# Padded q, k, v weight blocks and a changed order of VectorE's work in a fused attention and gated feed-forward kernel

## The chip, the cores and the metric

The kernel runs on one core of a Trainium2 chip. The metric is device time in microseconds (us), from the first to the last instruction of an execution with what lies around it; lower is better. Everything is fp32; matrix products read their operands as `float32r`, each operand split into a high and a low part, with three products (high x high, high x low, low x high) for one.

## The reference

The input has 2048 rows of 640. Both branches read the same layer-normed rows:

```python
xn = _layernorm(x)
qkv = (xn @ wqkv)                        # 32 heads of 20
# each row attends to W=8 rows: itself and 2, 4, ... 14 rows before it
logits = einsum("bhsd,bhswd->bhsw", q, kg) * scale; masked where the row is before the first
o = einsum("bhsw,bhswd->bhsd", softmax(logits), vg)
s = o @ wo
h = (xn @ w_gate) * (xn @ w_up)          # 1536 wide
g = silu(h @ w_down)
out = x + s * g
```

## The kernel before

The rows are spread over 128 partitions, 16 to each. A *unit* is one head group (four groups of 5 heads, two of 6) for one parity of rows; there are 12 units, numbered 0 to 11, and units 8 to 11 have 6 heads. `unit(u)` makes q, k and v of eight tiles with `qkv` (L317: 15 products of 300 or 360 columns in one PSUM bank, tag "q", four banks in rotation); ScalarE copies k and v to `kv` (L319) and q to `q` (L320); two times in a unit SyncE's queue issues copies of `kv` one partition on (L324), so that each partition has its neighbour's rows. `attention(u)` is a generator with VectorE's work: products of q and k (L351), sums (L354), mask, maximum, difference (L361); the exponential on ScalarE (L363, with the sum on VectorE behind it at L365); weighted values (L372) and their sums (L380, L383).

Between units stand *pieces* of the gated part. `gate_up(f, ch)` makes one block of 128 columns for a quarter of the rows: 15 products for `g` and 15 for `u`, of 512 columns each (L96), in PSUM tiles with two buffers each. ScalarE copies `g` to `gs` (L420). The product `hs = u * gs` on VectorE (L431) is put off: `finish` is kept in `unfinished` until `finish_piece()` is called, in the next piece, at a unit's second tile or by hand. The `u` bank is free for the next piece but one when its `hs` is done.

The order on each engine is that of the program. VectorE's is set by credits: each piece and each qkv tile calls `advance(budget)`, which takes steps of the running attention while its estimated costs fit. So the order of `hs` among attention's steps follows from where the calls stand. The number of pieces behind a unit is a line of the main loop: three, and four behind units 2 and 5, the rest at the end. A weight block's split (high part on ScalarE L86, low part on GpSimd L87) is called in the second piece of the block before.

Behind the units come the last pieces (f0 = 10 and f1 = 11) by hand, with what the next stage wants: `turn_pair` turns two tiles of attention's output (L491, L744 to L747), `hi_pair` and `lo_pair` split them in three parts (L764 on ScalarE, L768 on VectorE), `sums_wo` and `sum_w5` (L706) make combinations of the output weights, `split_t` and `split_w5` split these. `pair_product(p, j)` (L789) makes seven products for a pair, in places A, C and B (banks q, u, g): the first in place A, the second in place C, which takes the `u` bank of piece (f1, 2), the third again in A, after ScalarE has copied the first (L792). Then follow single output tiles (L96 in `out_proj`) and the down projection (L660).

Tiles lie one behind another in a partition's memory in the order in which they are first asked for; `skip(n)` puts n bytes between them. `wqh` and `wql` hold a group's weight block, five rows of 300 or 360 columns.

Of the kernel before, what the change touches and what calls it, by code (L numbers as in the profile page):

```python
# [12 lines left out]
F32R = mybir.dt.float32r  # L13
AF = mybir.ActivationFunctionType
# [5 lines left out]
P = 128  # L20
# [6 lines left out]
KD, KF = D // P, F // P  # L27
# [24 lines left out]
def kernel(  # L52
# [11 lines left out]
    nc = tc.nc  # L64
# [11 lines left out]
    def st(shape, tag, bufs, dt=F32):  # L76
        cnt[0] += 1
        return sb.tile(shape, dt, tag=tag, bufs=bufs, name=f"{tag}_{cnt[0]}")
# [19 lines left out]
    def skip(n):  # L98

        cnt[0] += 1  # L100
        sb.tile([P, n // 4], F32, tag=f"skip_{cnt[0]}", bufs=1, name=f"skip_{cnt[0]}")


    wq_raw, wq = {}, {}
# [10 lines left out]
    def split_wq(g, eng, ks=(0, KD)):  # L115
        c3 = 3 * GROUPS[g] * DH
        if g not in wq:
            wq[g] = st([P, KD, c3], "wqh", 1, F32R), st([P, KD, c3], "wql", 1, F32R)
        for k0, k1, t in wq_raw[g]:
            if ks[0] <= k0 < ks[1]:  # L120
                split(eng, t, wq[g][0][:, k0:k1], wq[g][1][:, k0:k1])
# [48 lines left out]
    eps_t = st([P, 1], "eps", 1)  # L170
# [92 lines left out]
    def scales(s0):  # L263
        mv, mr = stat[s0]
        nc.vector.tensor_copy(mr[:, 0, :], mv[:, :, 0])
        rstd(mv[:, :, 1], mr[:, 1, :], TPC)
        own[s0] = st([P, NQ, 2, TPC], "own", 2)
        nc.vector.tensor_mul(own[s0], mr.unsqueeze(1).to_broadcast([P, NQ, 2, TPC]),
                             quarter.unsqueeze(2).unsqueeze(3).to_broadcast([P, NQ, 2, TPC]))

    def spread(s0):

        p = pt([P, NQ, 2, TPC], "q", 4)
        nc.tensor.matmul(p, sel, own[s0], start=True, stop=True)
        spread_t[s0] = st([P, NQ, 2, TPC], "mrq", 2)
        nc.scalar.activation(spread_t[s0], p, AF.Copy)
# [51 lines left out]
    def attention(u):  # L328
        g, r = UN[u]
# [31 lines left out]
        nc.vector.tensor_sub(lg, lg, sm[:, 0, :].unsqueeze(2).to_broadcast([P, NE * nh, W]))  # L361
        yield 3 * small
        nc.scalar.activation(e, lg, AF.Exp, scale=SCALE)  # L363
        yield small
        nc.vector.tensor_reduce(out=sm[:, 0, :], in_=e, op=ALU.add, axis=AX.X)  # L365
        nc.vector.reciprocal(sm[:, 1, :], sm[:, 0, :])
# [42 lines left out]
    def gate_up(f, ch, between=(), amid=(), part=None):  # L409
        if part is None:  # L410
            pp = [pt([P, CH], "g", 2), pt([P, CH], "u", 2)]
            c = slice(0, CH)
        else:
            pp, c = part, slice(CH // 2, CH)
        last = (f, ch) == (KF - 1, NCH - 1)
        gate_up_half(f, ch, 0, pp[0], c)
        for act in amid:
            act()
        gs = st([P, CH], "gs", 2)
        nc.scalar.activation(gs, pp[0], AF.Copy)  # L420
        for act in between:
            act()
        share = (c.stop - c.start) / CH
        finish_piece()
        advance(PACE * 3.25 * share)
        gate_up_half(f, ch, 1, pp[1], c)

        def finish():
            hs = st([P, CH], "hs", 2)
            if not last:  # L430
                nc.vector.tensor_mul(hs, pp[1], gs)  # L431
            else:
                nc.scalar.activation(hs, pp[1], AF.Copy)
                nc.gpsimd.tensor_mul(hs, hs, gs)
            nc.sync.dma_start(h_scr[ch * TPC:(ch + 1) * TPC, :, f, :].rearrange("t p c -> p t c"),
                              hs.rearrange("p (t c) -> p t c", c=P))

        unfinished.append(finish)
        if last:
            finish_piece()  # L440
        advance(PACE * 3.25 * share)
# [3 lines left out]
    def finish_piece():  # L445

        while unfinished:
            unfinished.pop(0)()
# [289 lines left out]
    def turn_pair(p):  # L738
        y = pair_y[p] = st([P, 2, KD, P], "ot", 2)
        for i in range(2):  # L740
            turn(y[:, i], 2 * p + i)
        s1, s2, s4 = (pair_raw[p][:, i * KS:(i + 1) * KS] for i in range(3))
        a11, a12, a21, a22 = (y[:, i, k:k + KS] for i in range(2) for k in (0, KS))
        nc.vector.tensor_add(s1, a21, a22)  # L744
        nc.vector.tensor_sub(s2, s1, a11)
        nc.vector.tensor_sub(s4, a12, s2)
        nc.vector.tensor_sub(a21, a11, a21)  # L747
# [18 lines left out]
    def lo_pair(p, part):  # L766
        z, raw = pair_z[p, part]
        nc.vector.tensor_sub(z[1], raw, z[0].bitcast(F32))  # L768
# [35 lines left out]
            nc.sync.dma_start(s_scr[2 * p + 1], yb)  # L804


    skip(192)
    begin_unit(0)
    skip(192)
    mask = st([1, NE, W], "mask", 1)  # L810
    nc.gpsimd.memset(mask, 0.0)
    for i in range(NE - 1):
# [57 lines left out]
    load_xq(12, 3, xa)  # L870
    load_xq(15, 1, xd)
    scales(12)
    gate_up(0, 1, amid=(lambda: spread(8),))
    trans_q(8)
    trans_q(9)
# [56 lines left out]
    piece()  # L932
    for u in range(2, len(UN)):
        unit(u)
        for _ in range(3 + (u in (2, 5)) if u + 1 < len(UN) else len(pieces)):
            if len(pieces) == 1:
                load_wf(f1)
            piece()
# [28 lines left out]
    begin_wd()  # L967
    split_t("T1", wd_big[0], 4)
    split_t("T2", wd_big[0], 6)
    for i in range(3):  # L970
        lo_pair(0, i)
    gate_up(f1, 2)
    turn_pair(1)
    split_t("T3", wd_big[1], 4)
    split_t("T4", wd_big[1], 6)
    load_wd(0)
    load_wd(1)
    begin_wd()
    finish_piece()
    sum_w5()  # L980
    split_w5()
    gate_up(f1, 3)
# [148 lines left out]
```

## Time and profile before

| | |
|---|---|
| median of 3 runs | 778.97 us (778.11 to 779.29) |
| profiled execution, whole | 780.43 us |
| its span, first to last instruction | 778.6 us |
| TensorE busy | 767.9 us, 99% |
| VectorE busy | 697.3 us, 90% |
| ScalarE, GpSimd busy | 235.2 us, 150.1 us |
| mean granted TensorE clock | 0.995 |

A row of a timeline has the start, the length, engine, line, operation, output and inputs, shapes and count; in brackets the idle time before it and what ended it. Lengths of TensorE's products overlap, so starts are compared. Lines are those of the program above.

### The profile page before, as it was taken

How to read it: one execution, taken by the hardware profiler on the slowest of the kernel's cores; microseconds unless marked ns; L12 is line 12 of the kernel's file. 1: busy time of each engine (PE TensorE's matmuls, PEld its weight loads, DVE VectorE, ACT ScalarE, POOL GpSimd, SP SyncE). 2: the span in 40 equal slices, each digit the busy share in tenths (PEclk: the TensorE clock that was granted, in tenths of full speed). 3: DMA queues.
4: the chain of work that ended last, by engine and by line, in shares of the span. 5: the costliest groups of instructions: out<-in, count | busy, mean ns of one | idle time of the engine just before them, and what ended most of it. 6: DMA issues, size and time to landing. Idle time of an engine off the chain costs nothing.

```text
span 778.6 us, 11229 instructions
## 1 busy us (share of the span) xinstructions
PE 767.9 (99%) x4408; PEld 707.5 (91%) x4408; DVE 697.3 (90%) x731; ACT 235.2 (30%) x537; POOL 150.1 (19%) x114
## 2 busy tenths in 40 slices
PE   8999999999999999999999999999899999999997
PEld 7989899898989898989898989888799999999997
DVE  7899899999999999997999999999986787777775
ACT  4324312031112121312121212113455564444442
POOL 5200401022023101210204010034456720000000
PEclk9999999999999999999999999999999999999999
DMA  8552131321224122333032231444467674555533
GB/s 325 168 191 77 49 90 44 96 90 48 85 50 124 49 64 82 98 83 79 29 108 70 60 88 50 128 123 104 138 191 227 205 264 162 198 188 183 183 102 135
DMA packets 82252, 93.97 MB, mean 121 GB/s; under 512 B 23112, under 2 KB 63384, under 8 KB 82072
## 3 DMA queue, kind: packets, MB, share of 16 engines
q1 hardware_dynamic: 82200, 93.27, 38.7%
q8 instruction: 34, 0.56, 0.3%
q14 instruction: 18, 0.15, 0.1%
HBM read 55.84 MB, written 28.31 MB: 108 GB/s over the span
## 4 chain that ended last, share of the span: by engine, by line
PE 67%; DVE 24%; issue 5%; DMA 1%; ACT 1%; POOL 1%; DVEq 0%; SPq 0%; ACTq 0%; POOLq 0%
PE q L317 19%; PE q L660 11%; PE u L96 10%; PE g L96 10%; PE u L660 5%; PE q L96 5%; DVE t L351 4%; DVE t L380 4%; DVE t L372 4%; PE g L660 3%; DVE lg L354 2%; PE q L789 2%; DVE hs L431 2%; DVE xc L221 1%; PE u L789 1%
## 5 line engine op out<-in xcount | busy, mean ns | idle before, releaser
L96 PE MATMUL u<-xc,wf 128*128 128x512 f32 (+1 forms) x735 | 171.9, 386 | 0.4 <-DVE hs L431 0.4
L96 PE MATMUL g<-xc,wf 128*128 128x512 f32 (+1 forms) x735 | 172.1, 386 | 0.0
L317 PE MATMUL q<-wqh,xc 128*128 128x300 f32 (+1 forms) x960 | 161.6, 312 | 0.3
L96 PEld LDWEIGHTS u<-xc,wf 128*128 128x128 f32 x735 | 136.0, 188 | 28.0 <-DVE hs L431 0.8
L96 PEld LDWEIGHTS g<-xc,wf 128*128 128x128 f32 x735 | 135.7, 188 | 26.7
L317 PEld LDWEIGHTS q<-wqh,xc 128*128 128x128 f32 x960 | 147.0, 189 | 2.6 <-ACT wqh L86 0.4
L351 DVE TENSOR_TENSOR t<-q,kv 128x1600 f32<-128x1600 f32 (+1 forms) x48 | 98.7, 2055 | 6.2 <-DMA kv<-kv 6.2
L87 POOL TENSOR_TENSOR wf<-wraw,wf 128x256 fp32r<-128x256 f32 (+2 forms) x22 | 47.6, 2183 | 266.4 <-ACT wf L86 229.4
L372 DVE TENSOR_TENSOR t<-e,kv 128x1600 f32<-128x1600 f32 (+1 forms) x48 | 97.7, 2053 | 1.1
L354 DVE TENSOR_REDUCE lg<-t 128x80 f32<-128x1600 f32 (+1 forms) x48 | 92.6, 1929 | 1.1
L317 PE MATMUL q<-wql,xc 128*128 128x300 f32 (+1 forms) x480 | 87.2, 312 | 0.0
L420 ACT ACTIVATE gs<-g 128x512 f32<-128x512 f32 x48 | 28.6, 597 | 192.5 <-PE g L96 175.9
L380 DVE TENSOR_TENSOR t<-t,t 128x1600 f32<-128x1600 f32 (+1 forms) x36 | 78.8, 2190 | 1.0
L317 PEld LDWEIGHTS q<-wql,xc 128*128 128x128 f32 x480 | 75.4, 191 | 0.0
L319 ACT ACTIVATE kv<-q 128x200 f32<-128x200 f32 (+1 forms) x96 | 33.4, 348 | 125.2 <-PE q L317 125.2
L660 PE MATMUL q<-xc,wf 128*128 128x320 f32 x432 | 67.2, 309 | 0.0
L87 POOL TENSOR_TENSOR wql<-wraw,wqh 128x300 fp32r<-128x300 f32 (+4 forms) x14 | 35.3, 2539 | 165.6 <-ACT wqh L86 165.4
L660 PEld LDWEIGHTS q<-xc,wf 128*128 128x128 f32 x432 | 64.3, 188 | 0.0
L431 DVE TENSOR_TENSOR hs<-u,gs 128x512 f32<-128x512 f32 x47 | 32.0, 681 | 0.0
L87 POOL TENSOR_TENSOR xc<-wraw,xc 128x320 fp32r<-128x320 f32 (+1 forms) x22 | 26.2, 1193 | 28.5 <-ACT xc L86 25.4
L320 ACT ACTIVATE q<-q 128x100 f32<-128x100 f32 (+1 forms) x96 | 24.9, 259 | 0.0
L623 DVE TENSOR_TENSOR wf<-t,wf 128x768 fp32r<-128x768 f32 x16 | 15.3, 956 | 8.2 <-ACT wf L619 7.5
(259 smaller groups left out, 913.0 us busy)
## 6 DMA issues: line engine op xcount, KB each, us to landing
h_scr<-hs SPq DMA_DIRECT2D x48, 256.0 KB, 2.2
wraw<-in_wgu SPq DMA_DIRECT2D x12, 640.0 KB, 5.1
t<-h_scr SPq DMA_DIRECT2D x8, 768.0 KB, 7.0
hs<-s_scr SPq DMA_DIRECT2D x16, 320.0 KB, 3.5
gs<-in_x SPq DMA_DIRECT2D x16, 320.0 KB, 4.0
out<-q SPq DMA_DIRECT2D x14, 320.0 KB, 2.7
wraw<-h_scr SPq DMA_DIRECT2D x11, 384.0 KB, 5.9
wraw<-in_wd SPq DMA_DIRECT2D x12, 320.0 KB, 3.8
```

The lines of the kernel that those rows point to most:

```text
L87: eng.tensor_sub(lo, raw, hi.bitcast(F32))
L96: nc.tensor.matmul(acc, a, b, start=first and n == 0, stop=last and n == len(runs) - 1)
L317: nc.tensor.matmul(p, xT[(r * NE + i) // TPC][a][:, k, t0:t0 + P], wq[g][b][:, k], start=n == 0, stop=n == len(runs) - 1, skip_group_check ...
L319: nc.scalar.activation(kv_t[u][:, :, W - 1 + i, :], p[:, c:].rearrange("p (a c) -> p a c", a=2), AF.Copy)
L320: nc.scalar.activation(q_t[u][:, i, :], p[:, :c], AF.Copy)
L351: nc.vector.tensor_mul(t, q.rearrange("p i c -> p (i c)").unsqueeze(1).to_broadcast([P, 2, NE * c]), places(0, j))
L354: nc.vector.tensor_reduce(out=lg[:, :, j:j + 2].rearrange("p n a -> p a n"), in_=heads(t), op=ALU.add, axis=AX.X)
L372: nc.vector.tensor_mul(heads(t), pw, heads(places(1, j)))
L380: nc.vector.tensor_add(acc, acc, t)
L420: nc.scalar.activation(gs, pp[0], AF.Copy)
L431: nc.vector.tensor_mul(hs, pp[1], gs)
L660: nc.tensor.matmul(p, y[:, i, k], wd_t[name][k][:, l], start=new and r == 0, stop=r == len(runs) - 1, skip_group_check=True)
```

## The change

It has six edits.

1. The tiles `wqh` and `wql` get rows of 320 or 384 columns, of which 300 or 360 are used, so that each row of weights starts at a multiple of 256 bytes. The bytes skipped ahead are changed (192 and 192 to 32 and 160), which moves `q` and `kv` from 160 bytes past such a multiple onto one, and `wqh` and `wql` as well. The tile of edit 3 moves `lg`, `e` and `sm` to 32 bytes past one.
2. In `attention`, `finish_piece()` is called right behind the exponential.
3. An exponential of one column is run on ScalarE behind `scales(12)`.
4. The fourth piece is behind units 2 and 8, not 2 and 5.
5. `finish_piece()` for piece (f1, 2) is called right behind that piece, not behind `turn_pair(1)` and the splits.
6. `lo_pair(0, 2)` is moved behind that call.

```diff
     def split_wq(g, eng, ks=(0, KD)):
         c3 = 3 * GROUPS[g] * DH
         if g not in wq:
-            wq[g] = st([P, KD, c3], "wqh", 1, F32R), st([P, KD, c3], "wql", 1, F32R)
+            cols = -(-c3 // 64) * 64
+            wq[g] = [st([P, KD, cols], tag, 1, F32R)[:, :, :c3] for tag in ("wqh", "wql")]
...
         nc.scalar.activation(e, lg, AF.Exp, scale=SCALE)
+        finish_piece()
         yield small
...
-    skip(192)
+    skip(32)
     begin_unit(0)
-    skip(192)
+    skip(160)
...
     scales(12)
+    nc.scalar.activation(st([P, 1], "exp", 1), eps_t, AF.Exp)
     gate_up(0, 1, amid=(lambda: spread(8),))
...
-        for _ in range(3 + (u in (2, 5)) if u + 1 < len(UN) else len(pieces)):
+        for _ in range(3 + (u in (2, 8)) if u + 1 < len(UN) else len(pieces)):
...
-    for i in range(3):
+    for i in range(2):
         lo_pair(0, i)
     gate_up(f1, 2)
+    finish_piece()
+    lo_pair(0, 2)
     turn_pair(1)
     split_t("T3", wd_big[1], 4)
     split_t("T4", wd_big[1], 6)
     load_wd(0)
     load_wd(1)
     begin_wd()
-    finish_piece()
     sum_w5()
```

VectorE at the last pieces, before (L431 `hs` of pieces (f1, 1) and (f1, 2), L768 the low parts of pair 0, L491 to L747 `turn_pair(1)`):

```order
L431 TENSOR_TENSOR hs_4571<-u_4524,gs_4540 128x512
L768 TENSOR_TENSOR kv_4514<-ot_4516,kv_4514 128x640 x2
L768 TENSOR_TENSOR xc_4515<-kv_4412,xc_4515 128x768
L491 STREAM_TRANSPOSE ot_4616<-t_4504 128x640 x2
L744 TENSOR_TENSOR t_4504<-ot_4616 128x256
L745 TENSOR_TENSOR t_4504<-t_4504,ot_4616 128x256
L746 TENSOR_TENSOR t_4504<-ot_4616,t_4504 128x256
L747 TENSOR_TENSOR ot_4616<-ot_4616 128x256
L431 TENSOR_TENSOR hs_4634<-u_4583,gs_4599 128x512
```

The same place now (line numbers are two higher, and L770 is L768 of before):

```order
L433 TENSOR_TENSOR hs_4573<-u_4526,gs_4542 128x512
L770 TENSOR_TENSOR kv_4516<-ot_4518,kv_4516 128x640 x2
L433 TENSOR_TENSOR hs_4617<-u_4584,gs_4600 128x512
L770 TENSOR_TENSOR xc_4517<-kv_4415,xc_4517 128x768
L493 STREAM_TRANSPOSE ot_4621<-t_4506 128x640 x2
```

The `hs` of piece (f1, 2) has moved ahead of seven instructions: the third low part and the turning of pair 1.

ScalarE at the start of unit 6, before (`gs` of the last two pieces behind unit 5, the exponential of attention 5, then the evacuations of unit 6's tiles):

```order
L420 ACTIVATE gs_2423<-g_2406 128x512
L86 ACTIVATE wf_2425<-wraw_2359 128x1280
L420 ACTIVATE gs_2470<-g_2453 128x512
L363 ACTIVATE e_2385<-lg_2384 128x320
L319 ACTIVATE kv_116<-q_2503 128x2x100
L320 ACTIVATE q_2502<-q_2503 128x100
```

The same place now, from the `gs` of the third piece on:

```order
L422 ACTIVATE gs_2425<-g_2408 128x512
L86 ACTIVATE wf_2427<-wraw_2361 128x1280
L320 ACTIVATE kv_116<-q_2456 128x2x100
L321 ACTIVATE q_2455<-q_2456 128x100
L320 ACTIVATE kv_116<-q_2475 128x2x100
L321 ACTIVATE q_2455<-q_2475 128x100
L320 ACTIVATE kv_116<-q_2500 128x2x100
L321 ACTIVATE q_2455<-q_2500 128x100
L364 ACTIVATE e_2387<-lg_2386 128x320
L320 ACTIVATE kv_116<-q_2522 128x2x100
```

The fourth piece's `gs` is gone from here, unit 6 follows the third piece, and the exponential stands behind the evacuations of its first three tiles. At units 7 and 8 the exponential likewise stands behind two tiles and one.

ScalarE in the first part, before (the square root of `scales(12)`, the copy of `spread(8)`, `gs`):

```order
L200 ACTIVATE rstd_642<-mvo_112,eps_103 128x4
L276 ACTIVATE mrq_671<-q_669 128x32
L420 ACTIVATE gs_673<-g_652 128x512
L286 ACTIVATE xc_696<-ot_694 128x5x128
L286 ACTIVATE xc_696<-ot_702 128x5x128
```

The same place now:

```order
L201 ACTIVATE rstd_642<-mvo_112,eps_103 128x4
L875 ACT_TABLE_LOAD
L875 ACTIVATE exp_652<-eps_103 128x1
L277 ACTIVATE mrq_673<-q_671 128x32
L422 ACTIVATE gs_675<-g_654 128x512
```

The table load that stood ahead of the first attention's exponential stands here, with the new exponential behind it.

## The prediction

> **What bounds the kernel now.** I read the page's first part, then the waits of TensorE, then the timelines around its two longest stalls. Line 1 of the page gives busy time and share of the span by engine:
>
> ```profile
> PE 767.9 (99%) x4408; PEld 707.5 (91%) x4408; DVE 697.3 (90%) x731; ACT 235.2 (30%) x537; POOL 150.1 (19%) x114
> ```
>
> TensorE is never free for long, so the change can only gain where TensorE stands still or runs slowly, or by making a product shorter. Its waits between 500 and 600 us (total, times, longest), then VectorE's between 60 and 500 us:
>
> ```profile
> PE u L789 <- DVE hs L431: 2.4, 1, 2.4
> PE q L789 <- ACT o L792: 1.1, 1, 1.1
> ```
>
> ```profile
> DVE sm L365 <- ACT e L363: 7.4, 9, 2.2
> DVE t L351 <- DMA kv<-kv: 6.2, 1, 6.2
> ```
>
> TensorE's timeline (start, length, what, and in brackets the idle time before it and what ended it) at the first output products of the pairs:
>
> ```profile
> 553.61 1.04 PE L789 MATMUL q<-wf,kv 128*128 128x320 f32 x6
> 557.03 1.15 PE L789 MATMUL u<-xc 128*128 128x320 f32 x6 [2.38 <-DVE hs L431]
> 559.23 1.82 PE L789 MATMUL q<-xc 128*128 128x320 f32 x6 [1.05 <-ACT o L792]
> ```
>
> ```profile
> 563.07 1.04 PE L789 MATMUL q<-xc,kv 128*128 128x320 f32 x6
> ```
>
> Six products take 1.04 with the last one's own 0.31 at the end, so (1.04 - 0.31)/5 = 0.146 us from start to start. The first group should end its issue at 554.49 and the second starts at 557.03: 2.54 lost. The second should end at 557.91 and the third starts at 559.23: 1.32 lost. From 559.23 to 563.07 are 15 products (6, six single ones, 3) in 3.84 us where 15 x 0.146 = 2.19 were due: 1.65 lost. The windows (length, busy us and instructions of TensorE, weight loads, VectorE, ScalarE, GpSimd, then granted clock, DMA) say why:
>
> ```profile
> 552.60:556.00 3.40, 2.06 (x12) 1.59 (x10) 3.30 (x7) 0.00 (x0) 0.00 (x0) 1.00 0.86 282
> 556.00:559.40 3.40, 1.31 (x7) 1.05 (x8) 3.33 (x8) 1.99 (x6) 1.33 (x2) 1.00 0.27 81
> 559.40:562.80 3.40, 3.40 (x14) 3.40 (x15) 3.33 (x6) 2.44 (x6) 1.06 (x1) 0.50 0.26 77
> ```
>
> After 3.4 us in which TensorE was busy 1.31, the next 3.4 us ran at clock 0.50; after one with 2.06 busy the clock stayed 1.00. This place costs 2.54 + 1.32 + 1.65 = 5.5 us, the largest loss after the start-up.
>
> **The tail's order.** VectorE's timeline there (L768 low parts of the pairs, then 3.2 us of turning pair 1, L431 the piece's product, L706 the sum for the fifth block):
>
> ```profile
> 547.11 3.84 DVE L768 TENSOR_TENSOR kv<-ot,kv 128x640 fp32r<-128x640 f32 x2
> 550.87 2.32 DVE L768 TENSOR_TENSOR xc<-kv,xc 128x768 fp32r<-128x768 f32 x1
> ```
>
> ```profile
> 556.29 0.68 DVE L431 TENSOR_TENSOR hs<-u,gs 128x512 f32<-128x512 f32 x1
> 556.89 0.48 DVE L706 TENSOR_TENSOR wraw<-wraw 128x320 f32<-128x320 f32 x1
> ```
>
> ```profile
> 557.41 0.47 ACT L86 ACTIVATE kv<-wraw 128x320 fp32r<-128x320 f32 x1 [9.17 <-DVE wraw L706]
> ```
>
> The change puts `hs` of piece (f1, 2) ahead of the third low part and of `turn_pair(1)`: 556.29 - 550.87 = 5.4 us earlier, at about 550.9. Its product ended two half pieces before 553.61, at 553.61 - 2 x 3.40 = 546.8 (3.40 for a half piece is worked out below), and TensorE asks for the bank at 554.5, so the wait of 2.54 goes even if nothing else moves. What is late next is ScalarE: its queue stands at L86 until L706 is done (556.89 + 0.48 = 557.37), then does L86, `gs`, the last `hs` and the first L792, and TensorE starts 559.23 - 557.37 = 1.86 after L706. L706 comes earlier by the `hs` that no longer stands before it (556.89 - 556.29 = 0.6; in its new place it runs while the third low part would stand still for a GpSimd product, 2.32 long beside 0.82 to 0.95 elsewhere) and by VectorE's lead, which is the next term.
>
> **VectorE's lead.** VectorE's one long wait, 6.2 us, is for the neighbours' rows of unit 8. The fourth piece, now behind unit 8, makes PE and ScalarE reach unit 8 that much sooner, and five exponentials (attention 6 to 10) now have an `hs` in the hole behind them, which fills about 0.6 each of the 7.4 in the row above. Both move VectorE forward, and the next thing that stops it is again the neighbours' rows. For the last unit:
>
> ```profile
> 486.16 1.56 SPq L324 DMA_DIRECT2D kv<-kv  x2
> ```
>
> ```profile
> kv<-kv SPq DMA_DIRECT2D x4, 315.0 KB, 3.2
> ```
>
> ```profile
> 492.79 2.15 DVE L351 TENSOR_TENSOR t<-q,kv 128x1920 f32<-128x1920 f32 x1
> ```
>
> The rows land at 486.16 + 3.2 = 489.4 and VectorE begins at 492.79: 3.4 us later than it could. With TensorE's own shift of 1.2 (below) the lead is at most 2.2. By the new order no later `hs` then stands on VectorE before its product is done, so none takes the lead away. I take 2.2; its ends are 0 and 3.4. Then L706 ends at 557.37 - 0.6 - 2.2 = 554.6 and the third group may start at 554.6 + 1.86 = 556.4. TensorE asks for it at 559.23 - 2.54 - 1.32 + 1.2 = 556.6. So neither wait is left, and no stretch at half clock: **-5.5**. With no lead at all the third group starts at 558.6, waits 2.0 and may keep the slow stretch: then only 0.6 to 2.3 is gained there.
>
> **The piece moved from unit 5 to unit 8.** TensorE, then ScalarE, then VectorE, around unit 6 (g and u of the fourth piece at 263.28 and 267.21, unit 6 at 270.74 to 287.43):
>
> ```profile
> 263.28 3.56 PE L96 MATMUL g<-xc,wf 128*128 128x512 f32 x15
> 267.21 3.69 PE L96 MATMUL u<-xc,wf 128*128 128x512 f32 x15 [0.37 <-DVE hs L431]
> 270.74 0.84 PE L317 MATMUL q<-wqh,xc 128*128 128x300 f32 x5
> ...
> 287.43 3.58 PE L96 MATMUL g<-xc,wf 128*128 128x512 f32 x15
> ```
>
> ```profile
> 278.12 0.47 ACT L363 ACTIVATE e<-lg 128x320 f32<-128x320 f32 x1 [10.28 <-DVE lg L361]
> 278.50 0.32 ACT L319 ACTIVATE kv<-q 128x200 f32<-128x200 f32 x1
> ```
>
> A half piece undisturbed lasts 15 x 0.227 = 3.40, so u should start at 266.68: 0.53 is lost, because the `hs` two pieces back is late. In the new order unit 6 stands between, and its 16.7 us cover that `hs`: **-0.5**. But unit 6 itself now starts at 263.28, its tiles 16.69/8 = 2.09 apart, and the exponential of attention 5 stands on ScalarE behind tile 2, with the evacuation of tile 3 behind it. VectorE has the same rows ahead of that exponential as before, so it starts at 278.12 again; tile 3's bank is free at about 278.12 + (278.50 - 278.12) + 0.5 = 279.0. There are four banks, so tile 7 needs it, at 263.28 + 7 x 2.09 = 277.9: **+1.1**. Ends: 0 if VectorE is a little early, 3 if it is late by two more. For the pieces after it, `hs` of the moved piece follows one product more of attention 6:
>
> ```profile
> 294.38 1.82 DVE L351 TENSOR_TENSOR t<-q,kv 128x1600 f32<-128x1600 f32 x1
> ```
>
> It starts at 296.24 - 0.6 = 295.6 and ends at 296.3; u of the piece two on starts at 263.28 + 16.7 + 1.1 + 17.0 (five half pieces) = 298.1. That holds by 1.8 us: nothing. The other `hs` of units 6 to 8 hold by 2 to 15 by the same count.
>
> **The early exponential.** It sets the table between the third square root and `mrq`, on ScalarE's queue; VectorE's scaling waits for `mrq`, and TensorE for the low part that ends this chain:
>
> ```profile
> 50.52 0.18 ACT L276 ACTIVATE mrq<-q 128x32 f32<-128x32 f32 x1
> ```
>
> ```profile
> 51.76 1.18 DVE L221 TENSOR_SCALAR xc<-xc,mrq 128x160 f32<-128x160 f32 x4
> ```
>
> ```profile
> 65.16 0.96 PE L317 MATMUL q<-wqh,xc 128*128 128x300 f32 x5
> ```
>
> ```profile
> 92.18 1.28 ACT L363 ACT_TABLE_LOAD   x1
> ```
>
> `mrq` would start at 50.52 + 0.1 + 1.28 + about 0.2 for one column (it has 0.18 for 32) = 52.1 and end at 52.3 where VectorE wants it at 51.76: 0.5 late. VectorE has no gap from there to 65.1, when TensorE resumes after a short stall at 65.16, so **+0.5** (ends 0 and 1.7). The Trainium skill (ScalarE: Activation LUTs, What ACT_TABLE_LOAD costs) gives 1.28 for the load and 1.38 more for a drain; by that the term would be +1.9, but here the exponential at 92.18 + 1.28 follows at once. The 1.3 us saved at 92 help nobody, since the second exponential stands behind a split on ScalarE that TensorE's pace sets:
>
> ```profile
> 129.11 1.27 ACT L86 ACTIVATE wf<-wraw 128x1280 fp32r<-128x1280 f32 x1
> 130.28 0.46 ACT L363 ACTIVATE e<-lg 128x320 f32<-128x320 f32 x1
> ```
>
> **The padding.** Products by shape, mean ns of one:
>
> ```profile
> L96 PE MATMUL u<-xc,wf 128*128 128x512 f32 x705 | 167.8, 390 | 0.4 <-DVE hs L431 0.4
> L317 PE MATMUL q<-wqh,xc 128*128 128x300 f32 x640 | 102.8, 304 | 0.3
> L660 PE MATMUL q<-xc,wf 128*128 128x320 f32 x432 | 67.2, 309 | 0.0
> L317 PE MATMUL q<-wqh,xc 128*128 128x360 f32 x320 | 58.7, 328 | 0.0
> ```
>
> Those with 512 and 320 columns already read at multiples of 256 bytes (or nearly all do): 81 ns for 192 columns, 0.42 each. That line gives 301 for 300 columns and 326 for 360; they take 304 and 328. If alignment is the whole difference, 960 x 3 + 480 x 2 = 3.8 us go; but 0.146 for 320 columns and 2.09/15 = 0.139 for 300 differ by 7 ns, about what 20 columns at 0.42 are worth, which leaves nothing. Ends -3.8 and +0.5; I take **-0.4**. On VectorE I take nothing: its tiles move too (`q` and `kv` to multiples of 256, `lg`, `e` and `sm` off them by 32), and L351's rows read `kv` at four different places with the same 1.82.
>
> **The sum.** -5.5 - 0.5 + 1.1 + 0.5 - 0.4 = -4.8; the tail has only 0.2 to spare against VectorE's chain, for which I give 0.5 back: -4.3. The profiled execution took 780.43 with a span of 778.6, so it would take 776.1 with a span of 774.3. The three runs have a median of 778.97, and from it 774.7.
>
> **The rivals.**
> - *Padding speeds the products by what their lengths show*: -3.8 instead of -0.4, so 771.3. For it the 304 and 328, against it the starts 0.139 apart. 0.13.
> - *VectorE has no lead at the tail*, because a queue ahead (a store of `o` before the neighbours' rows of the next unit, which the new order has at unit 9) holds it as long as now: 0.6 gained there and the half clock stays, -0.6 - 0.5 + 1.1 + 0.5 - 0.4 = +0.1, so 779. 0.10.
> - *The half clock stays though the waits go.* Its stretch then has another cause, and the gain is 1.65 less: 776.4. 0.07. The Trainium skill (TensorE: Matmul & The Clock Gate, HAM oscillation) asks for idle gaps of some 3.4 us before the clock falls; by that rule the waits of 2.5 and 1.3 would not be the cause, while the windows above show the fall after 1.31 busy of 3.40.
> - *Slower: VectorE falls behind between units 5 and 8*, where the fourth piece used to give it 6.8 us. It decides from waits of 5.4 us in units 6 to 8 (those 1.1 included). If a GpSimd split stretches VectorE by 2.2 more (the two low parts at 547.11, 3.84 for 1.64) ahead of two of the exponentials, tile 7 waits 3.3 in each of two units, and each brings a slow stretch of 1.65: 9.9 instead of 1.1, +4.5, so 783.5. For it speaks ScalarE's wait of 10.28 for that very exponential; against it that the next two have two tiles' room. 0.12.
>
> **How the numbers follow.** The forecast as summed has 0.58: 774.7. A difference of 0.2% (1.6 us) is about what a measurement of this kernel can tell from no change. Faster by more are the forecast, the padding and the half clock, 0.78; the same is the tail without lead, 0.10; slower 0.12. The range goes from 771.5, most of the way to the padding's case, to 778.2, which takes in small leads; what lies outside is the slower case and about half of two rivals.
>
> **What would show it.** Right: no wait of u L789 for `hs`; `hs` near 549 to 551; the clock 1.00 between 552 and 563; TensorE's group of unit 6 with one wait near 278 on q for ScalarE; VectorE's wait of 6.2 for `kv` at unit 8 split or moved to units 9 to 11; the low part at 65.1 later by 0.5. Wrong: new waits of q L317 for `kv` evacuations above 2 us, or of u L96 for `hs` between 280 and 385; the 300-column products with a mean clearly below 304.

## The result and the profile after

| | before | changed |
|---|---|---|
| median, 14 runs each | 778.96 us (777.99 to 781.88) | 777.62 us (776.34 to 781.81) |
| ratio | | 0.9985, 95% interval 0.9974 to 0.9997 |
| profiled execution, whole | 780.43 us | 778.27 us |
| its span | 778.6 us | 776.4 us |
| forecast | | 774.7 us (span 774.3) |

The kernel is 1.3 us faster by the medians, 2.2 by the spans of the profiled executions (1.4 of these are the start-up's, below), where 4.3 were forecast. The first line of the page, and the shares of the engines in the chain that ended last, changed and then before:

```profile
PE 763.9 (98%) x4408; PEld 702.7 (91%) x4408; DVE 696.7 (90%) x731; ACT 235.4 (30%) x538; POOL 147.0 (19%) x114
```

```profile
DVE 49%; PE 38%; issue 9%; DMA 1%; ACT 1%; SPq 1%; DVEq 0%; ACTq 0%
```

```profile
PE 67%; DVE 24%; issue 5%; DMA 1%; ACT 1%; POOL 1%; DVEq 0%; SPq 0%; ACTq 0%; POOLq 0%
```

TensorE is busy 4.0 us less, three times what the medians show, and the chain that ended last now runs for half of its length through VectorE, where it ran mostly through TensorE.

TensorE's waits of the changed kernel (total, times, longest; those of the start-up left out):

```profile
PE q L791 <- ACT o L794: 3.1, 1, 3.1
...
PE q L318 <- ACT q L321: 0.9, 1, 0.9
PE u L96 <- DVE hs L433: 0.7, 2, 0.4
PE q L318 <- DVE xc L289: 0.5, 2, 0.3
```

The wait for `hs` at the pairs (2.4) is gone, as forecast, and the next one, for ScalarE's first copy L794, has gone from 1.1 to 3.1. TensorE's timeline there:

```profile
550.88 1.04 PE L791 MATMUL q<-wf,kv 128*128 128x320 f32 x6
551.76 1.04 PE L791 MATMUL u<-xc 128*128 128x320 f32 x6
555.90 1.97 PE L791 MATMUL q<-xc 128*128 128x320 f32 x6 [3.10 <-ACT o L794]
...
562.17 0.31 PE L791 MATMUL g<-wqh,kv 128*128 128x320 f32 x1
```

The pairs begin at 550.88 where they began at 553.61, 2.73 sooner, and the second group follows at once. The third could be issued at 551.76 + 6 x 0.146 = 552.64 and starts at 555.90: 3.26 lost. From there to 562.17 stand 24 products, 6.27 us where 3.50 were due: 2.77 lost at half clock. So the place costs 6.0 us; before, it cost 5.5. The windows (columns as in the prediction; the granted clock is the third number from the end) show the slow stretch behind the wait:

```profile
552.20:555.60 3.40, 0.60 (x5) 0.34 (x3) 3.30 (x8) 1.52 (x4) 0.87 (x2) 0.91 0.71 261
555.60:559.00 3.40, 3.10 (x11) 3.10 (x12) 3.30 (x6) 2.30 (x6) 1.52 (x1) 0.50 0.26 77
559.00:562.40 3.40, 3.40 (x16) 3.40 (x16) 2.33 (x5) 1.78 (x5) 2.27 (x2) 0.59 0.00 0
562.40:565.80 3.40, 3.40 (x25) 3.40 (x24) 2.88 (x5) 0.44 (x1) 0.99 (x2) 1.00 0.16 59
```

VectorE and ScalarE at that place, from their timelines:

```profile
548.13 0.68 DVE L433 TENSOR_TENSOR hs<-u,gs 128x512 f32<-128x512 f32 x1
...
553.56 0.48 DVE L708 TENSOR_TENSOR wraw<-wraw 128x320 f32<-128x320 f32 x1
```

```profile
554.08 0.47 ACT L86 ACTIVATE kv<-wraw 128x320 fp32r<-128x320 f32 x1 [8.58 <-DVE wraw L708]
...
555.41 0.44 ACT L794 ACTIVATE o<-q 128x320 f32<-128x320 f32 x1
```

`hs` of piece (f1, 2) stands at 548.13 instead of 556.29. L708 (L706 before) ends at 554.04 instead of 557.37, and ScalarE, whose queue has stood at L86 for 8.58 us, releases the third group 1.86 after it, as before. The place is set by VectorE's chain to L708; TensorE only arrives earlier and waits longer. It begins the pairs 2.73 sooner than before and leaves the place 2.2 sooner, and those 2.2 are the difference of the spans.

**Where TensorE's 2.73 us come from.** The start-up gave 1.44: the block of `g` that began at 15.36 begins at 13.92. These two windows (before, then changed) show clock 0.52 in one execution and 1.00 in the other:

```profile
10.00:13.40 3.40, 3.25 (x14) 3.28 (x15) 2.98 (x10) 0.77 (x2) 0.00 (x0) 0.52 1.00 378
```

```profile
10.00:13.40 3.40, 3.22 (x25) 3.25 (x26) 3.19 (x12) 2.11 (x8) 0.30 (x1) 1.00 1.00 387
```

That is no part of the change: `e5_tail` (below), which is the kernel before up to the last pieces, ran this window at 1.00 and began that block at 14.00. Its VectorE is sooner by the same 1.4 in every attention, the last one starting at 491.43 instead of 492.79. So the start-up moves both engines alike, and the differences to the profile before, TensorE's and VectorE's, have some 1.4 us in them that no edit made.

The padding gave 4.0. The products by shape:

```profile
L318 PE MATMUL q<-wqh,xc 128*128 128x300 f32 x640 | 101.3, 300 | 1.6 <-ACT q L321 0.9 <-DVE xc L289 0.5 <-DVE rstd L204 0.2
L318 PE MATMUL q<-wqh,xc 128*128 128x360 f32 x320 | 57.2, 322 | 0.0
```

They take 300 and 322 ns where they took 304 and 328. From start to start, the mean over all products that follow without a wait is 136.8 ns where it was 138.5 (300 columns), and 160.4 where it was 165.3 (360): 960 x 1.7 + 480 x 4.9 = 4.0 us. Against these stand 0.5 in unit 0, 1.1 in unit 6 and three waits for `hs` near 219, 257 and 332 us, 0.7 + 0.4 + 0.6 with the products behind them; the loss of 0.6 at 267 is gone. -1.44 - 4.0 + 0.5 + 1.1 + 1.7 - 0.6 = -2.74, which is the 2.73.

### The profile page after: what moved, and what is told of

It is laid out like the page before. It is cut to its first block, busy times and chain, and to the rows that moved or that the text cites. A ratio compares the mean times of both kernels' runs of the same rounds, so it can differ in the third digit from the quotient of the medians.

```text
span 776.4 us, 11230 instructions
## 1 busy us (share of the span) xinstructions
PE 763.9 (98%) x4408; PEld 702.7 (91%) x4408; DVE 696.7 (90%) x731; ACT 235.4 (30%) x538; POOL 147.0 (19%) x114
## 4 chain that ended last, share of the span: by engine, by line
DVE 49%; PE 38%; issue 9%; DMA 1%; ACT 1%; SPq 1%; DVEq 0%; ACTq 0%
PE q L662 11%; DVE t L352 11%; DVE t L374 10%; DVE t L382 9%; DVE lg L355 6%; PE u L662 5%; PE q L96 5%; PE q L318 4%; PE g L96 3%; DVE hs L433 3%; PE g L662 3%; PE u L96 3%; PE q L791 2%; PE u L791 1%; DVE xc L222 1%
## 5 line engine op out<-in xcount | busy, mean ns | idle before, releaser
L318 PE MATMUL q<-wqh,xc 128*128 128x300 f32 (+1 forms) x960 | 158.5, 308 | 1.6 <-ACT q L321 0.9
L318 PEld LDWEIGHTS q<-wqh,xc 128*128 128x128 f32 x960 | 144.3, 188 | 4.3 <-ACT q L321 1.2
L87 POOL TENSOR_TENSOR wf<-wraw,wf 128x256 fp32r<-128x256 f32 (+2 forms) x22 | 47.1, 2161 | 229.0 <-ACT wf L86 229.0
L382 DVE TENSOR_TENSOR t<-t,t 128x1600 f32<-128x1600 f32 (+1 forms) x36 | 84.7, 2353 | 1.1
L318 PE MATMUL q<-wql,xc 128*128 128x300 f32 (+1 forms) x480 | 85.2, 307 | 0.0
L318 PEld LDWEIGHTS q<-wql,xc 128*128 128x128 f32 x480 | 73.6, 188 | 0.0
L87 POOL TENSOR_TENSOR wql<-wraw,wqh 128x300 fp32r<-128x300 f32 (+4 forms) x14 | 33.0, 2377 | 203.1 <-ACT wqh L86 203.1
```

What stands on the lines that cost most here:

```text
L87: eng.tensor_sub(lo, raw, hi.bitcast(F32))
L318: nc.tensor.matmul(p, xT[(r * NE + i) // TPC][a][:, k, t0:t0 + P], wq[g][b][:, k], start=n == 0, stop=n == len(runs) - 1, skip_group_check ...
L382: nc.vector.tensor_add(acc, acc, t)
```

## The experiments

Ratios are to the kernel before on the same chip, with 95% intervals. Theory A throughout: VectorE's chain sets when the third group of pair 0 may start; what TensorE saves ahead of it is waited away there, and a longer wait brings a longer stretch at half clock. Line numbers of the kernels differ by a few.

### Edit 1 alone, and all but edit 1

`e1_pad` is the kernel before with the padded blocks and `skip(32)`, `skip(160)`; `e2_nopad` the changed kernel with `st([P, KD, c3], ...)` and both `skip(192)` again.

> The kernel before with edit 1 alone (rows of the weight blocks padded, the bytes skipped ahead changed). Theory A (the tail is set by VectorE's chain, which TensorE waits for, and a longer wait there brings a longer stretch at half clock): TensorE reaches the first product of the pairs 4.0 us sooner (1.7 ns less from start to start for 960 products of 300 columns, 4.9 ns less for 480 of 360, as the changed kernel's trace shows), VectorE is ahead by about 2 (its last wait, for rows of unit 8, ends with TensorE's work on that unit), so the waits at the pairs grow from 3.9 to about 5.8 us and the stretch at half clock from 1.65 to about 3 us lost: the time changes by -2.1 + 1.4 = -0.7, about 778.3. Rival B (what products save is saved at the end too): 4.0 less, 775. Rival C (padding does nothing, the earlier start of the pairs is the luck of the start-up): 779 and the same starts.

> The changed kernel without edit 1 (weight rows of 300 and 360 columns and the former skips again, edits 2 to 6 kept). Theory A: TensorE reaches the pairs 4.0 us later than in the changed kernel, at about 554.9, and asks for the third group at 556.8; VectorE's chain to L708 hangs on its own work and not on TensorE, so the third group may start at 556 to 556.4: no wait of more than 0.5, no stretch at half clock, and the end is 0.9 later by TensorE and 2.9 sooner by the clock: 775.6, faster than the changed kernel though its products are longer. Rival B: 4.0 more than the changed kernel, 781.6. Rival C: the same as the changed kernel, 777.6, with the same wait of 3.

`e1_pad`: 782.19 us, 1.0035 (1.0023 to 1.0046), slower than before. `e2_nopad`: 775.07 us, 0.9949 (0.9934 to 0.9965), faster than the changed kernel although its products are longer. In `e1_pad` TensorE is 4.25 us ahead at the last pieces (their first product at 481.31 where it was at 485.56), of which 1.5 from the start-up, and then VectorE is late with an `hs` among those pieces already:

```profile
PE u L96 <- DVE hs L432: 3.2, 2, 2.8
PE u L790 <- DVE hs L432: 2.3, 1, 2.3
```

```profile
521.66 6.55 PE L96 MATMUL u<-xc,wf 128*128 128x512 f32 x15 [2.79 <-DVE hs L432]
```

The half piece behind that wait takes 6.55 where 3.56 is usual: a slow stretch more. Theory A had VectorE ahead by 2 us here and the time at 778.3; VectorE is late instead. One of its products of q and k stands beside a split on GpSimd and takes 4.93 where the same product takes 2.15 before (463.28):

```profile
460.77 4.93 DVE L352 TENSOR_TENSOR t<-q,kv 128x1920 f32<-128x1920 f32 x1
```

```profile
460.74 2.94 POOL L87 TENSOR_TENSOR wf<-wraw,wf 128x1280 fp32r<-128x1280 f32 x1 [42.60 <-ACT wf L86]
```

L707 (L706 before) ends at 558.98 instead of 557.37, though the start-up was some 1.4 sooner, and the third group starts at 560.84, again 1.86 behind it. That TensorE waits for VectorE is as theory A has it; that the splits fall elsewhere in VectorE's work once TensorE is sooner, and make VectorE itself later, was not foreseen, and with it neither the place nor the sign. In `e2_nopad` the three groups follow each other:

```profile
554.15 1.04 PE L790 MATMUL u<-xc 128*128 128x320 f32 x6
555.10 1.14 PE L790 MATMUL q<-xc 128*128 128x320 f32 x6
```

The third starts at 555.10, 0.8 sooner than in the changed kernel, without a wait, and no slow stretch follows. The 0.8 are VectorE's: L707 ends at 553.24 where L708 ends at 554.04.

```profile
552.75 0.49 DVE L707 TENSOR_TENSOR wraw<-wraw 128x320 f32<-128x320 f32 x1
```

In the changed kernel a product of q and k, at 463.02, takes 4.27 beside a split that GpSimd begins at 462.32; in `e2_nopad` it takes 2.15. That is the largest difference between the two on VectorE; smaller ones, beside other splits, go both ways. Edits 2 to 6 without the padding bring 3.9 us, the padding takes 2.6 of them back. So the forecast without its term for the padding, 774.7 + 0.4 = 775.1, is what edits 2 to 6 measured.

### TensorE kept busy in its wait

```diff
-        for r, (y, w) in enumerate(runs):
-            nc.tensor.matmul(b, y, w, ...)
+        for n in range(4 if (p, j) == (0, 1) else 1):
+            for r, (y, w) in enumerate(runs):
+                nc.tensor.matmul(b, y, w, ...)
```

> The changed kernel with work that serves nothing in TensorE's wait at the pairs: the six products of the second group of pair 0 are issued four times, each time from the start of the bank, so 18 more products of 0.147 us, 2.6 us. If the stretch at half clock comes from TensorE standing still there (theory A), the third group starts when it did (556.0 after the same chain through VectorE), the next 24 products run at 0.147 instead of 0.267, and 2.9 us go: 774.8. If the clock falls for another reason (rival D: load of all engines, or a place in the program), the time stays at 777.6 with the same stretch at 0.50. If the third group does not wait for VectorE's chain but for TensorE's own issue (rival B), 2.6 come on top: 780.2.

775.96 us, 0.9958 (0.9942 to 0.9974): 1.7 us less than the changed kernel by adding 18 products; 2.2 by the spans (774.2). The third group starts at 556.15. The windows:

```profile
552.20:555.60 3.40, 3.40 (x24) 3.22 (x22) 3.32 (x7) 1.27 (x3) 0.72 (x1) 1.00 0.78 283
555.60:559.00 3.40, 2.94 (x20) 2.85 (x20) 3.26 (x7) 3.12 (x7) 1.69 (x2) 1.00 0.22 67
```

The clock stays at 1.00. The slow stretch came from TensorE standing still, and the third group's start did not hang on TensorE.

### L708 sooner

```diff
     finish_piece()
+    sum_w5()
     lo_pair(0, 2)
...
     begin_wd()
-    sum_w5()
     split_w5()
```

> The changed kernel with the one subtraction of sum_w5 (L708, 0.48 us) moved on VectorE ahead of the third low part and of the turning of pair 1, right behind hs of piece (f1, 2). ScalarE's queue stands at the split of its result for 8.6 us now. Theory A: L708 is done at 549.2 instead of 554.0, the first copy L794 follows the first group at once, and the third group starts at about 552.6 without the wait of 3.1 and without the slow stretch: 6.4 us sooner there. VectorE's next results then limit TensorE: the low part of pair 1 (L770, wf, done at 561.8 and 0.5 later by the moved subtraction) is asked for at 563.5 - 6.4 = 557.1, so TensorE stands there for 5 us instead, with a slow stretch behind it: 1.3 less at the end, minus or plus the difference of the slow stretches, 775 to 778. If VectorE's chain is not what holds the third group (rival B), the wait of 3.1 stays and the time is 777.6.

778.72 us, 0.9993 (0.9982 to 1.0005): no gain over before, above theory A's 775 to 778, and 1.1 behind the changed kernel's median, although the profiled span, 775.6, is 0.8 shorter. The third group starts at 552.28 without a wait; the next results of VectorE take its place, and ahead of them stands the turning of pair 2:

```profile
PE q L791 <- DVE xc L770: 2.4, 1, 2.4
PE q L791 <- DVE hs L800: 1.4, 1, 1.4
```

```profile
558.14 0.41 DVE L749 TENSOR_TENSOR ot<-ot 128x256 f32<-128x256 f32 x1
...
559.40 0.82 DVE L770 TENSOR_TENSOR xc<-ot,xc 128x640 fp32r<-128x640 f32 x1
...
560.53 1.22 DVE L770 TENSOR_TENSOR wf<-t,wf 128x768 fp32r<-128x768 f32 x1
```

L749 is the end of that turning. The first of the two waits, which ends at 560.27, is for the low part of pair 1 at 559.40 (`xc`); the second ends at 562.21, for a sum (`hs`, L800) that stands behind the low part at 560.53 (`wf`).

So it is all of VectorE's work there that binds, not one subtraction.

### Single edits

`e5_tail` is the kernel before with edits 5 and 6; `e6_nomove` the changed kernel without edits 1 and 4; `e7_noexp` without edits 1 and 2; `e10_noearly` without edits 1 and 3.

> The kernel before with edits 5 and 6 alone (hs of piece (f1, 2) right behind the piece, the third low part behind it). Theory A: the wait of 2.4 for that hs goes, but the third group still hangs on VectorE's chain to L706, which gains only the 0.6 of the hs that stood before it and up to 0.6 of a low part that is no longer stretched: the third group starts at 558.0 to 558.6 where TensorE asks for it at 555.4, so one wait of 2.6 to 3.2 takes the place of 2.4 + 1.1 and the stretch at half clock stays, 1.65 to 2.9 lost: 778 to 779.5. Rival P (the wait was that hs's own, and with it goes the whole loss of 5.5): 773.5.

> The changed kernel without edits 1 and 4 (no padding, the fourth piece behind unit 5 again; edits 2, 3, 5, 6 kept). Theory A with VectorE's lead from the moved piece: VectorE again waits for the rows of unit 8 until 370 or 371, is 2 to 3 us later at the pairs than without edit 1 alone, the third group waits 2.5 to 3.5 and a stretch at half clock follows: 778 to 780 against the 775.1 of the kernel with the piece moved, though the wait of 1.0 in unit 6 is gone. Rival L (the lead comes from the holes behind the exponentials that edit 2 fills): 774 to 775.

> The changed kernel without edits 1 and 2 (no padding, hs not called behind the exponential; edits 3 to 6 kept). Against the kernel without edit 1, three holes of 0.54 us on VectorE come back, those of attentions 6, 7 and 8 (at 9 and 10 an hs stood there in the kernel before too), 1.8 us with the hs that filled them. Theory A with the queue of stores: the rows of unit 9 stand in SyncE's queue behind the store of attention 8's output, so what VectorE loses ahead of it isn't made up in its wait there but moves that wait: VectorE is 1.8 later to the end, the third group of the pairs starts at 556.9 instead of 555.1, TensorE waits 1.8, and a stretch at half clock may follow: 777 to 778.5. Rival W (the wait for the rows of unit 9 swallows it): 775.1.

> The changed kernel without edits 1 and 3 (no padding, no early exponential). Edit 3's price by the prediction: 0.5 us on TensorE near 65 us. Without edit 1 TensorE sets the end, so it should show there: 774.6 against 775.1, with the stall before the last tile of that unit down from 0.3 to at most 0.1. Rival: VectorE, later by 1.5 at the first exponential (table load at 92), is held to the end: 775.1 to 776.5 with a wait of the third group.

`e5_tail`: 778.20 us, 0.9995 (0.9980 to 1.0010). Edits 5 and 6 alone are worth nothing measurable; of the prediction's -5.5 they are the part without VectorE's lead, for which it said 0.6 to 2.3. TensorE's wait of 2.4 for `hs` became one of 3.1 for the copy behind L706, which ends at 555.42, 0.6 sooner than before once the start-up's 1.36 is taken off:

```profile
PE q L789 <- ACT o L792: 3.1, 1, 3.1
```

```profile
554.94 0.48 DVE L706 TENSOR_TENSOR wraw<-wraw 128x320 f32<-128x320 f32 x1
```

`e6_nomove`: 778.64 us, 0.9999 (0.9988 to 1.0010). Without the moved piece the third group waits again, and the rival L falls:

```profile
PE q L790 <- ACT o L793: 3.1, 1, 3.1
```

`e7_noexp`: 775.21 us, 0.9969 (0.9950 to 0.9988), the median that of `e2_nopad`; rival W was right. Only two holes come back, not three: 0.54 us in attention 7 and 0.59 in attention 9; at 6, 8 and 10 an `hs` stands in the hole without edit 2 as well. VectorE's waits for the neighbours' rows, without and with edit 2:

```profile
DVE t L351 <- DMA kv<-kv: 5.7, 2, 5.6
```

```profile
DVE t L351 <- DMA kv<-kv: 6.2, 2, 5.6
```

The first hole makes VectorE 0.5 later at unit 8 and is gone behind the wait of 5.6 at unit 9; the second is taken up at unit 11, where the kernel with edit 2 waits 0.6 for rows. Four of the twelve runs took 779.1 to 780.6 and eight 774.6 to 775.4; the profiled one is of the eight. What the four met isn't shown, so that edit 2 is worth nothing is shown for the eight alone.

`e10_noearly`: 774.74 us, 0.9945 (0.9931 to 0.9958), against 775.07 with the early exponential. Unit 0's second half took 8.86 us on TensorE (57.98 to 66.84) where it took 9.37 with it (55.42 to 64.79): 0.51, edit 3's price. Its profiled execution has the start-up's half clock (0.58 between 10.0 and 13.4 us), which is why its rows stand later.

### VectorE's chain shortened

`e8_best` is the changed kernel, padding kept, with `sum_w5()` as in `e4_w5`, the turning of pair 2 behind the low parts of pair 1, and attention's stores issued behind the copies of the neighbours' rows:

```diff
-                nc.sync.dma_start(o_scr[...], o[...])
+                stores.append((o_scr[...], o[...]))
...
+def flush():
+    while stores:
+        nc.sync.dma_start(*stores.pop(0))
```

with `flush()` at the end of a unit's tiles and at the start of a piece. Why the stores: in the changed kernel SyncE's queue, and VectorE behind it, had this at unit 9:

```profile
405.22 1.02 SPq L390 DMA_DIRECT2D o_scr<-o  x2
406.34 1.73 SPq L325 DMA_DIRECT2D kv<-kv  x2
```

```profile
DVE t L352 <- DMA kv<-kv: 5.4, 1, 5.4
```

ScalarE had written the last of these rows at 404.25; their copy stood behind the store of attention 8, which waited for VectorE, which then waited for the copy. `e9_final` has the turning of pair 2 one product later and leaves edit 3 out.

> The changed kernel with three more moves, padding kept: attention's stores are issued behind the copies of the neighbours' rows of the unit that runs; sum_w5 stands right behind hs of piece (f1, 2); the turning of pair 2 stands behind the low parts of pair 1, between products 4 and 5 of pair 0. Theory A (VectorE's chain sets the end, so the padding's 4 us were lost in waits and slow clock): VectorE is 1.9 earlier from unit 9 on, L708 is done at about 547.5, the low part of pair 1 at about 556 instead of 561.8, before TensorE asks for it at 557.1; TensorE starts the pairs at 550.9 and has neither a wait nor a slow stretch there: 6 us less than the changed kernel, 771 to 772.5. Rival B (the tail has another bound, or the padding's gain isn't there): 775 or more.

> The kernel of e8_best with two edits: the turning of pair 2 one place later on VectorE, behind product 5 of pair 0 and its sum (L807), which frees the buffer that ScalarE's first copy of pair 1 waits for; and without edit 3 (no early exponential). Theory A: the wait of 1.4 before the second group of pair 1 goes, and 0.5 at the low part in unit 0, whose scaling no longer stands behind the table load: the profiled span goes from 771.1 to about 769.3, the time to 771 to 773, with TensorE busy without a wait above 0.5 from the pairs on. Rival: the low parts of pair 2 come too late for TensorE (asked for at 564.8 and due at 563 to 565), a wait of up to 2 there, 773 to 775.

`e8_best`: 774.59 us, 0.9943 (0.9921 to 0.9965), 773.11 at best, short of theory A's 771 to 772.5; the third group starts at 551.78, and one wait is left, for a copy whose buffer is freed by a sum that stood behind the turning of pair 2:

```profile
PE q L796 <- ACT o L799: 1.4, 1, 1.4
```

`e9_final`: 771.52 us, 0.9904 (0.9890 to 0.9917), granted clock 1.000 in the profiled execution: as theory A has it, and faster than both kernels. The copy now stands ahead of the store:

```profile
403.33 1.87 SPq L325 DMA_DIRECT2D kv<-kv  x2
405.30 1.17 SPq L397 DMA_DIRECT2D o_scr<-o  x2
```

VectorE's wait at unit 9 is halved, not gone:

```profile
DVE t L352 <- ACT gs L427: 2.7, 1, 2.7
```

The view names ScalarE's `gs`, which ended last by the profile, but this product reads q and kv; the rows of unit 9 landed at 406.82, 0.12 before VectorE's start at 406.94, and in the changed kernel the same 0.12 lie between 410.46 and 410.58.

### The padding and the moved piece once more

`e13_final_nopad` is `e9_final` without edit 1, `e14_final_nomove` without edit 4.

> The kernel of e9_final without edit 1 (rows of 300 and 360 columns, the former skips). There TensorE has no wait from the pairs on, so what products save should be saved at the end: theory A says 960 x 1.6 + 480 x 4.9 ns = 3.9 us more than e9_final, 775.4, no wait at the pairs. Rival V (VectorE still sets the end of e9_final, and TensorE has the 3.9 us to spare): 771.5. Rival D (padding's effect on the products is given back elsewhere, in VectorE's reading of q and kv): anything from 772 to 774.

> The kernel of e9_final with the fourth piece behind unit 5 again (edit 4 undone). The wait of 0.9 in unit 6 goes (1.1 us with what follows), and 0.5 comes back before u of the next piece. VectorE waits for the rows of unit 8 again and is some 5 us later from unit 8 on; in e9_final it has 2.2 idle at 551 and about 1 to spare at the low part of pair 1, so TensorE waits there for about 1.7: theory A 772 to 774, with one wait of 1 to 3 at the pairs and perhaps a slow stretch. Rival (with the stores out of the way VectorE's lead isn't needed): 770.9, no wait at the pairs.

`e13_final_nopad`: 774.21 us, 0.9930 (0.9913 to 0.9947). Where VectorE does not hold the tail, the same padding that cost 2.6 us is worth 2.7 by the medians, 2.0 by the ratios (the two were compared with the kernel before on different chips). Of its 3.9, some 1.2 go to small waits for `hs` that the longer products don't meet; `e9_final` has them, `e13_final_nopad` doesn't:

```profile
PE u L96 <- DVE hs L438: 0.7, 2, 0.4
```

`e14_final_nomove`: 771.40 us, 0.9891 (0.9873 to 0.9909), the same as `e9_final`; the rival was right on the wait, not on the gain. VectorE is 2.3 later at unit 11 (488.61 where 486.28) and has that to spare. The wait of unit 6 is gone, the pairs begin 1.4 sooner, and 1.2 of that is lost again in small delays at the pairs. With the stores out of the way the moved piece is not needed.

### Which half of the padding

`e11_rows` has the padded rows and the former skips, `e12_skips` the new skips and rows of 300 and 360; one run each, for the products' lengths.

> The changed kernel with half of edit 1: the rows of the weight blocks padded to 320 and 384 columns, the skips as in the kernel before, so that every row of weights starts 192 bytes past a multiple of 256, and q and kv 160 past. Read: mean time from start to start of the products of 300 and 360 columns (138.5 and 165.3 ns before, 136.8 and 160.4 changed). Theory R (rows whose distance is a multiple of 256 bytes): 136.8 and 160.4. Theory S (the start of a row at a multiple of 256): 139 and 165. Theory G (the place of q and kv, which VectorE reads at the same time): 138.5 and 165.3.

> The changed kernel with the other half of edit 1: the skips changed, so that q, kv and the first row of weights start at a multiple of 256 bytes, but rows of 300 and 360 columns without padding, which then start at 0, 176, 96, 16, 192 (300 columns) and 0, 160, 64, 224, 128 (360) past one. Theory R: 138.5 and 165.3 as before. Theory S: only the row at 0 is quicker, by 2 and 5 ns. Theory G: 136.8 and 160.4.

From start to start `e11_rows` has 136.7 and 166.7 ns, `e12_skips` 137.8 and 165.7: each half helps the 300 columns, neither the 360, and no theory of the three holds for both shapes. Something else moved, which I had not looked for: tiles that lie behind these, among them the `wf` blocks that TensorE loads as weights for the 512-column products. By the program's layout they start at a multiple of 256 bytes before and in the changed kernel, 192 bytes past one in `e11_rows` and 64 in `e12_skips`, while the `xc` rows that stream past them start at a multiple in all four. The rows of the three, in this order:

```profile
L96 PE MATMUL u<-xc,wf 128*128 128x512 f32 x705 | 168.1, 390 | 0.9 <-DVE hs L433 0.7
```

```profile
L96 PE MATMUL u<-xc,wf 128*128 128x512 f32 x705 | 169.4, 392 | 0.1
```

```profile
L96 PE MATMUL u<-xc,wf 128*128 128x512 f32 x705 | 172.2, 395 | 0.0
```

From start to start that is 227 ns (a half piece of 15 in 3.40 us), 229.0 and 233.3. In `e12_skips` these products alone cost TensorE 1410 x 6.3 = 8.9 us, so the two times, 779.63 and 780.96 us, say nothing of the padding.

## Why the prediction was wrong, step by step

**The padding, -0.4: the step that failed.** The sum took it as a small term of its own that comes on top of the tail's -5.5. It was mis-sized: on TensorE it measured -4.0, just past the end of its range. And it was no term that can be added: it brings TensorE to the pairs ahead of VectorE, so the tail's gain, which needed TensorE to ask for the third group (556.6) no sooner than VectorE's chain allows it (556.4), went with it. On the time the padding measured +2.6 (777.62 against the 775.07 of `e2_nopad`), and without it the rest of the sum came out (775.1 forecast, 775.07 measured; to be so near is luck, since its terms have errors of some tenths).

On the size: the mean lengths, 304 and 328 against a line through 512 and 320 columns, had said 3.8. I overruled them by the starts of 300 columns alone and left the 360 columns, where most of it is (480 x 4.9 = 2.4), without that test. The padded products take 300 and 322 by their rows, a little under what that line gives for their lengths (301 and 326): the alignment was the whole difference and somewhat more. A mean clearly below 304 was one of the prediction's own signs of being wrong.

**The tail, -5.5: right in the chain that it named, wrong in what meets it.** The third group was forecast to start at 556.4 and started at 555.90; `hs` was forecast "near 549 to 551" and stood at 548.13; L706's end at 554.6 was 554.04. These hits are in part luck, since 1.4 of them are the start-up's. TensorE was to ask for the group at 556.6 and asked at 552.64: 1.4 sooner by the start-up, which moves VectorE as well, 4.0 by the padding, which the shift of 1.2 left out, and 1.6 later by waits that I had not foreseen. The sentence that "the tail has only 0.2 to spare against VectorE's chain" was in the prediction, and I applied 0.5 of it to the sum and none to the rivals. A term that brings TensorE sooner to a place which VectorE sets is not added; it is lost, and here paid for at half clock. `e2_nopad` and `e13_final_nopad` show it from two sides: with VectorE arriving last the padding costs, without that it saves.

**The rival of the padding, 771.3, had the right size and the wrong end** for the same reason: 3.8 added behind a sum with 0.2 to spare. What it would have been worth with the tail free, `e13_final_nopad` shows.

**The half clock.** The rival that it has another cause is out by `e3_fill`. The Trainium skill (TensorE: Matmul & The Clock Gate, HAM oscillation) puts the gap that it takes at some 3.4 us. The traces do not agree, and here they decide: a wait of 3.10 was enough, in the window with 0.60 busy, and before the change waits of 2.38 and 1.05 with one group of products between them.

**VectorE's lead, 2.2.** L708 is 3.33 sooner; without the start-up's 1.36 and the 0.6 of the `hs` that no longer stands before it, 1.4 are left for the lead. In `e2_nopad`, where L707 ends at 553.24, the same count gives 2.2, as forecast: the padding took 0.8, with a product beside a split as the largest difference. Where the lead comes from was half wrong. Of the five holes that edit 2 was to fill it fills two (`e7_noexp`), and the waits for rows behind them take both up. The moved piece gives the lead (`e6_nomove`). The rival's queue, a store ahead of the rows of unit 9, was there to the letter and cost VectorE 2 us, but didn't take the lead away.

**The piece moved: -0.5 and +1.1 were right.** ScalarE and TensorE in unit 6:

```profile
276.90 0.47 ACT L364 ACTIVATE e<-lg 128x320 f32<-128x320 f32 x1 [7.71 <-DVE lg L362]
```

```profile
277.80 0.96 PE L318 MATMUL q<-wqh,xc 128*128 128x300 f32 x5 [0.92 <-ACT q L321]
```

0.92, and 0.1 to 0.2 in the products behind it. The stall before `u` at 267 is gone. The piece that was to hold by 1.8 holds; three others wait 0.3 to 0.4. Those near 219 and 257 us lie ahead of unit 6, where I had counted none; this one I had counted as safe by 2 or more:

```profile
334.31 1.89 PE L96 MATMUL u<-xc,wf 128*128 128x512 f32 x7 [0.31 <-DVE hs L433]
```

**The early exponential, +0.5: right**, 0.51 by `e10_noearly`, and the 1.3 saved at 92 helped nobody: there VectorE starts attention 1 sooner by 1.9 with edit 3 than without, and attention 2 at the same distance from TensorE in both.

**Slower by VectorE between units 5 and 8:** no wait above 0.9 there; the rival is out.

## What to carry to other kernels

Before adding a gain on one engine to the sum, ask at the next place where it meets the other engine which of them arrives last; a gain of the earlier one ends there, and a longer wait can cost the clock as well. So order the edits: first shorten the chain that arrives last (here a queue with a store ahead of a copy, and work that wasn't due yet ahead of work that was), then speed up the other engine: the same padding cost 2.6 us before that and saved 2.0 to 2.7 after it. When the mean length of an instruction and its distance from start to start disagree, test both on every shape before choosing one.

## What the runs showed of the hardware that I had not expected

TensorE's products of one shape differ in length with where their fp32r operands start in memory, the one that streams through and the one loaded as weights: 360 columns take 160.4 ns with all rows at multiples of 256 bytes and 166.7 with the rows as far apart but 192 bytes past one (`e11_rows`); 512 columns take 227.0 with the weights at a multiple and 233.3 with them 64 bytes past one (`e12_skips`). Other tiles moved with them in these runs, so that it is the operand's own start is the simplest reading and not isolated. The Trainium skill (SBUF — State Buffer, Operand start alignment) gives the element's 4 bytes as what is legal and says that its runs timed nothing. These are times for it, though not a rule: `e11_rows` and `e12_skips` don't yield one.

The start-up has a stretch at half clock in some executions (0.52 before, 1.00 in `e5_tail`, in the same window of the same work), worth 1.36 us on TensorE and VectorE alike: two single profiles can differ by that with nothing changed there.
